# Down of the later chunks as three float32r products, up and down in quarters, third weight parts kept in DRAM

## The chip, the cores and the metric

The kernel runs on one core of a Trainium2 chip. The metric is device time in microseconds, lower is better. The engines are TensorE (PE, its weight loads shown as PEld), VectorE (DVE), ScalarE (ACT), GpSimd (POOL) and SyncE (SP), which issues nearly all DMAs. Each executes its own instructions in order and waits on semaphores for the others. SBUF is the on-chip memory, PSUM holds the sums of TensorE in banks.

## The reference

A mixture of two blocks: an mLSTM cell over 768 positions for 4 batches and 8 heads of 40, and then a GELU layer with 2048 hidden features.

```python
for t in range(S):                       # cell; B, H, S, D = 4, 8, 768, 40
    m_new = np.maximum(f_gate[:, :, t] + m, i_gate[:, :, t])
    f_stab = np.exp(f_gate[:, :, t] + m - m_new)
    i_stab = np.exp(i_gate[:, :, t] - m_new)
    m = m_new
    C = f_stab[..., None, None] * C + i_stab[..., None, None] * np.einsum('bhd,bhe->bhde', vt, kt)
    n = f_stab[..., None] * n + i_stab[..., None] * kt
    h_tilde = np.einsum('bhde,bhe->bhd', C, qt)
    denom = np.maximum(np.abs(np.einsum('bhd,bhd->bh', n, qt)[:, :, None]), 1.0)
    y[:, :, t] = sigmoid(o_gate[:, :, t]) * h_tilde / denom
x = y.transpose(0, 2, 1, 3).reshape(B * S, H * D)      # 3072 x 320
h = x @ w_in                                           # 320 x 2048  ("up")
g = 0.5 * h * (1.0 + erf(h / sqrt(2)))
return g @ w_out                                       # 2048 x 320  ("down")
```

## The kernel before

The 768 positions are cut into six chunks of 128, so a chunk has 4 x 128 = 512 tokens, a tile of 128 for each batch. Within a chunk the cell is computed by matrices: scores of q and k (`scores_two`, into tile `ps`), weighted by exponents of the gates (tile `W`: the row `M_d` is loaded by `load_M`, masked on POOL by `mask`, turned into exponents on ACT by `weights`), what comes from earlier chunks (`read_two`, tile `pf`, and the new state in `update_two`), and the values (`values`, tile `ph`). `finish` divides by the denominator, `turn_y` transposes y into `px` and `split_x` makes the three parts of the layer's input. q and k come through a DRAM copy (`copy_chunk`, `kq_d`) and `load_blocks`, and are transposed on DVE by `turn_k` and `turn_q`.

A float32 matmul takes two records in the profile. Up of the later chunks avoids it: x and w_in are each split into a high and a low part of type float32r plus a third one, and the sum of three products (high x high, low x low, rest x sum) stands for the float32 product. The third weight part, high + low, is made anew on DVE for each chunk (`join_weight`, L827) into a few buffers (`w_mid`). `up` does this in four pairs: `pair(0)`, `pair(1)`, `rest(0)`, then `pair(2)`, `pair(3)`, `rest(1)`. 16 blocks of 128 hidden features come out as tiles `pu`, and `out` applies gelu on ACT (L1036) into `g`.

Down of chunks 1 to 4 is one Strassen-like step: seven products of half the size instead of eight, in float32 (`down_steps`, matmuls at L1137), with sums of g's halves made on DVE (`hidden_sums`, L864 to L866, and `sum_late`, L1163), sums of the weights made once (`weight_sum`) and adds of the results (L1148). Down of the first chunk is a plain float32 product (`first_down_steps`, L1116). Down of the last chunk is already three float32r products (`LastDown`, matmuls at L991): gelu writes `g_whole`, ACT makes the high part (`split_hi`, L974), DVE the low one and the rest (`split_lo`, L977 and L978).

The order of the work is written out by hand. A step is a letter with a number; `play` walks through the words of an order and emits the step's instructions on all engines. `FRONT` holds the first two chunks of the cell, the conversion of the weights (`K` is `conv_one` on ACT, `J` is `conv_two` on DVE, which also fetches the next piece) and the first down (`F`, one row of w_out for all four tiles). Then, for each chunk, `up` is emitted as a whole, and `DOWN` mixes the products `F` of its down with the steps of the next chunk's cell. Since every engine runs in order, a word's place says what stands behind it. SP is a queue too: a DMA that waits for a buffer to be free holds all later ones.

Of the kernel before, what the change touches and what calls it, by code (L numbers as in the profile page):

```python
# [16 lines left out]
P = 128  # L17
# [14 lines left out]
    K V3 X1 J K r F J h8 h9 F F K F F F F F J K X2 G3 F F J K J F J K Y3 K B10 R1 X3 F p R2 J R3 F F J F F"""  # L32
DOWN = """
    M0 F Z F L3 W0 M1 W1 S0 C0 F F h0 Q2 F K2 G1 D3 B3 V0 G2 M2 W2 M3 W3 V1 K3 Q3 F G0 S2 Y0 G3 C2 h2 F
    F Y1 X0 V2 V3 F N F j R0 Y2 Y3 X1 F F X2 R1 F R2 X3 R3 F"""
# [3 lines left out]
def kernel(  # L39
# [34 lines left out]
    HELD = 7  # L74
    WP = 512
# [20 lines left out]
    w_out = const.tile([P, NF, DM], F32, name="w_out", tag="w_out")  # L96
# [28 lines left out]
    right_d = dram.tile([P, DFF // P // 2, DM // 2], F32, name="right_d")  # L125
# [95 lines left out]
    def warm(n):  # L221
        cold = ps_h.tile([P, P], F32, name="cold", tag="h")
        for _ in range(n):
            nc.tensor.matmul(cold, w_out[:, 0, 0:P], w_out[:, 0, 0:P], start=True, stop=True, skip_group_check=True)

    def fill(n):
        cold = ps_h.tile([P, P], F32, name="cold", tag="h")
        for i in range(n):
            r = quarters[i % 4]
            nc.tensor.matmul(cold[r, 0:D1], w_out[:, 0, r], w_out[:, 0, 0:D1], start=True, stop=True, skip_group_check=True)  # L230

    nc.vector.memset(w_out[:, 0, 0:P], 0.5)
# [116 lines left out]
    for f in range(NF):  # L349
        pieces.append(([w_src["out"][f * P:(f + 1) * P, :]], w_out[:, f, :]))  # L350
# [53 lines left out]
    later_loads = []  # L404
# [20 lines left out]
    class Cell:  # L425


        def __init__(self, c):
            self.c = c

            self.engine = nc.vector if c < 2 else nc.gpsimd
            self.finished, self.turned, self.reads = [], [], []
            self.qT, self.kT, self.vw, self.far, self.hs, self.px = {}, {}, {}, {}, {}, {}
# [43 lines left out]
        def load_last(self, b):  # L477

            self.by_block = fars[0].tile([P, NP, 2, L], F32, name="blocks3", tag="x_lo", bufs=1)
            for r in (32, 96):  # L480
                nc.gpsimd.memset(self.by_block[r:r + 32], 0.0)
            load_blocks(self.c * B + b, self.by_block)

        def last_M(self, b):
            load_M(self.c * B + b, self.before.t[:, 0:HF, P:2 * P])

        def turn_half(self, b, i):
            src = by_block if b < B - 1 else self.by_block
# [7 lines left out]
        def turn_q(self, b):  # L496
            self.turn_half(b, 1)
            if b < B - 2:
                load_blocks(self.c * B + b + 1, by_block)
            if self.c < NCH - 1 and b < B - 1:  # L500
                self.weigh_values(b)

        def load_next(self):
            if self.c + 1 < NCH:
                load_blocks((self.c + 1) * B, by_block)
            if self.c + 2 < NCH:
                copy_chunk(self.c + 2)

        def weigh_last(self, b):
# [36 lines left out]
        def scores_two(self, b0):  # L546

            two_b = (b0, b0 + 1)
            ps = [[pool.tile([P, NP, L], F32, name="ps", tag=tag) for hip in range(2)] for pool, tag in ((ps_mm, "a"), (ps_tr, "tr"))]
# [15 lines left out]
        def carry(self, b):  # L565
# [35 lines left out]
            self.read(b)  # L601

        def read_two(self, b0):

            c, two_b = self.c, (b0, b0 + 1)
            banks = self.banks = [ps_h.tile([P, H + NP, D1], F32, name="pf", tag="h") for _ in range(2)]
# [8 lines left out]
        def update_two(self, b0):  # L615

            c, two_b, banks = self.c, (b0, b0 + 1), self.banks
            if c + 1 < NCH:
                for i, b in enumerate(two_b):
                    vw = self.vw.pop(b)  # L620
                    for p in range(NP):
                        for hip in range(2):
                            nc.tensor.matmul(banks[i][used[hip], H + p, :], kb[turn_of(c * B + b)][:, 2 * p + hip, 0:D],  # L623
                                             vw[:, 2 * p + hip, :], start=True, stop=True)
            for i, b in enumerate(two_b):
                if b == B - 1:
                    self.far[b] = qb[2].rearrange("p h d -> p (h d)")[:, 0:H * D1].rearrange("p (h d) -> p h d", d=D1)
                else:
                    self.far[b] = fars[0].tile([P, H, D1], F32, name="far", tag="hs", bufs=2)
# [4 lines left out]
                if c + 1 < NCH:  # L634
                    st, d = state[b][:, :, 0:D1], dec[:, c - 1, b * NP:(b + 1) * NP].unsqueeze(2).to_broadcast([P, NP, D1])
                    nc.gpsimd.tensor_tensor(out=st, in0=st, in1=d, op=OP.mult)
                    for r in used:
                        nc.vector.tensor_tensor(out=st[r], in0=st[r], in1=banks[i][r, H:H + NP, :], op=OP.add)
                self.read(b)

        def read(self, b):

            self.reads.append(b)
            if self.c > 1 and self.reads.count(b) == 2:
                if b == 0:
                    load(self.c * B + NQ, 1, 3)
                else:
                    later_loads.append(lambda: load(self.c * B + b + NQ, 1, 3))

        def values(self, b):  # L650
# [3 lines left out]
            pool, tag = (ps_mm, "a") if self.c > 1 else (ps_h, "h")  # L654
# [5 lines left out]
            if self.c > 1 and b > 0:  # L660
                later_loads.append(lambda: load_M(n + NW))
            self.read(b)
# [6 lines left out]
        def finish(self, b):  # L669
# [3 lines left out]
            if self.c > 1:  # L673
                nc.scalar.activation(out=den, in_=hs[:, :, D], func=AF.Abs)
                nc.gpsimd.tensor_scalar(out=den, in0=den, scalar1=1.0, scalar2=None, op0=OP.max)
            if self.c < 2:
                nc.vector.scalar_tensor_tensor(out=y, in0=y, scalar=1.0, in1=hs[:, :, 0:D], op0=OP.add, op1=OP.mult)
            else:
                nc.gpsimd.tensor_tensor(out=y, in0=hs[:, :, 0:D], in1=y, op=OP.mult)
            if self.c < 2:  # L680
# [16 lines left out]
        def turn_y(self, b):  # L697
            n, t = self.c * B + b, slice(b * L, (b + 1) * L)
            if self.c > 0:
                px = ps_tr.tile([P, NX + 1, L], F32, name="px", tag="tr")  # L700
            else:
                px = ps_mm.tile([P, NX + 1, L], F32, name="px", tag="b")
# [18 lines left out]
            else:  # L721
                later_loads.append(lambda: load(n + NLD, 3, 4))
# [10 lines left out]
    HF, HT, HD = NF // 2, TG // 2, DM // 2  # L733

    Bm = [[lambda j, e=e, n=n: w_out[:, HF * e + j, HD * n:HD * (n + 1)] for n in range(2)] for e in range(2)]
    w_sums, parts, fars, w_hi, w_lo, w_mid = [], {}, [], {}, {}, {}
    T = {1: lambda j: w_sums[0][:, j, :], 2: lambda j: w_sums[1][:, j, :], 3: Bm[0][1]}
# [80 lines left out]
    def join_weight(i):  # L825
        w_mid[i] = raw.tile([P, 2, WP // 2], F32R, name="w_in_mid", tag="pow") if i % 5 in (1, 4) else w_f(F32R, "w_mid")
        nc.vector.tensor_tensor(out=w_mid[i], in0=w_hi[i], in1=w_lo[i], op=OP.add)  # L827

    def weight_sum(n):
        if n == 1:  # L830
            both = fars[0].tile([P, 2, HF, HD], F32, name="w_sums", tag="w_sums")
            w_sums.extend([both[:, 0], both[:, 1]])
        x, y = {1: (Bm[0][1], Bm[0][0]), 2: (Bm[1][1], T[1]), 3: (Bm[1][1], Bm[0][1])}.get(n) or (Bm[1][0], T[2])
        if n == 4:

            parts = {}

            def t4(j):
                if j // 3 not in parts:
                    parts[j // 3] = raw.tile([P, 3, HD], F32, name="t4", tag="pow" if j > 5 else "sig")  # L840
                return parts[j // 3][:, j % 3, :]

            T[4] = t4

        def step(j):
            nc.vector.tensor_tensor(out=T[n](j), in0=x(j), in1=y(j), op=OP.subtract)

        return [lambda j=j: (step(j), step(j + 1)) for j in range(0, HF, 2)]

    class Hidden:  # L850


        def __init__(self, summed):
# [416 lines left out]
```

## Time and profile before

| | us |
|---|---|
| median of 3 runs (lowest, highest) | 455.23 (454.81, 456.16) |
| span of the profiled execution | 453.3 |
| granted TensorE clock, mean | 1.000 |
| first down starts (chain) | 85.9 |
| chunk 1, 2, 3, 4, 5 start (first up matmul) | 121.0, 190.4, 260.3, 329.8, 397.0 |
| seven float32 products of a chunk, L1137 (chain) | 31.6 |
| three float32r products of the last chunk, L991 (chain) | 26.3 |
| one chunk of up (chain) | 26.5 |

The times of runs are medians of whole executions. The span is that of one profiled execution, from the first to the last instruction, and all durations are taken from it. A row of the groups gives a line, an engine, the tiles, how many there were, the busy time and the mean of one. A row of the timeline gives start, duration and what was merged; consecutive instructions of one engine overlap a little, so that the distance of two starts is shorter than a duration.

### The profile page before, as it was taken

To read this page: it belongs to the slowest core of one execution; us is meant where nothing else is said; L and a number is where in the kernel's file an instruction comes from. 1 tells how busy PE (TensorE), PEld (TensorE's weight loads), DVE (VectorE), ACT (ScalarE), POOL (GpSimd) and SP (SyncE) were. 2 spreads that over 40 slices of the span, in tenths; PEclk is the share of its full clock that TensorE was granted. 3 is DMA by queue.
4 is the path that set the end of the run, shared out by engine and by line. 5 is a ranking of instruction groups with operands and counts; after the bars stand their busy time and mean duration, and the time that the engine had idled before them with its cause. 6 is when DMAs were issued, how large, how long until landed. Compare 5 with 4: busy or idle time off the path is not lost.

```text
span 453.3 us, 13140 instructions
## 1 busy us (share of the span) xinstructions
PE 444.2 (98%) x5440; PEld 393.2 (87%) x5440; DVE 314.7 (69%) x672; ACT 238.2 (53%) x541; POOL 77.3 (17%) x117
## 2 busy tenths in 40 slices
PE   8899999999999999999999999999999999999996
PEld 7787888777788999988999988899988899988996
DVE  8797688877269688735578656488645577699940
ACT  4999999764231791221791203693203594247701
POOL 3002030000100443101433101533001513000000
PEclk9999999999999999999999999999999999999999
DMA  7999874886265644149834139942019930200001
GB/s 156 235 211 229 191 212 88 240 246 162 75 153 124 108 63 111 45 92 212 137 55 111 45 57 221 126 88 23 25 47 208 151 81 4 88 30 0 1 1 59
DMA packets 174876, 51.12 MB, mean 113 GB/s; under 512 B 154752, under 2 KB 168352, under 8 KB 174816
## 3 DMA queue, kind: packets, MB, share of 16 engines
q1 hardware_dynamic: 174496, 49.95, 50.5%
q8 instruction: 43, 0.70, 0.6%
q10 hardware_dynamic: 320, 0.33, 0.2%
q14 instruction: 17, 0.14, 0.1%
HBM read 45.47 MB, written 10.03 MB: 122 GB/s over the span
## 4 chain that ended last, share of the span: by engine, by line
PE 88%; ACT 6%; DVE 2%; DMA 1%; SPq 1%; issue 1%; DVEq 0%; ACTq 0%
PE po L1137 27%; PE pu L1021 23%; PE po L1116 8%; PE pu L1032 6%; PE po L991 6%; PE ph L659 3%; PE ps L557 3%; ACT W L465 2%; PE pu L810 2%; PE pf L612 2%; PE px L706 2%; PE pu L877 2%; PE pf L623 1%; SPq L151 1%; DMA bits<-in_moe_w_in_dram 1%
## 5 line engine op out<-in xcount | busy, mean ns | idle before, releaser
L1036 ACT ACTIVATE g<-pu 128x512 f32<-128x512 f32 x64 | 32.2, 618 | 81.2 <-PE pu L1032 81.2
L1137 PE MATMUL po<-w_out,g 128*128 128x160 f32 x512 | 74.4, 302 | 0.0
L1137 PEld LDWEIGHTS po<-w_out,g 128*128 128x128 f32 x512 | 70.1, 190 | 1.9 <-ACT g L1036 1.3
L1021 PE MATMUL pu<-x_hi,w_in_hi 128*128 128x512 f32 x160 | 39.0, 387 | 0.0
L465 ACT ACTIVATE W<-W,aT 128x128 f32<-128x128 f32 x128 | 38.6, 388 | 0.1
L439 POOL TENSOR_SCALAR_AFFINE_SELECT W<-W 128x1024 f32<-128x1024 f32 (+2 forms) x20 | 25.0, 1254 | 77.9 <-DMA W<-M_d 77.3
L1137 PE MATMUL po<-w_sums,sums 128*128 128x160 f32 x256 | 36.9, 302 | 0.0
L1137 PEld LDWEIGHTS po<-w_sums,sums 128*128 128x128 f32 x256 | 35.0, 190 | 0.4
L1116 PE MATMUL po<-w_out,g 128*128 128x320 f32 x128 | 34.9, 432 | 0.0
L1021 PEld LDWEIGHTS pu<-x_hi,w_in_hi 128*128 128x128 f32 x160 | 29.5, 189 | 5.7 <-ACT g L1036 1.3
L1116 PEld LDWEIGHTS po<-w_out,g 128*128 128x128 f32 x128 | 24.1, 190 | 9.7
L563 DVE TENSOR_TENSOR W<-ps,W 128x256 f32<-128x256 f32 (+1 forms) x48 | 18.1, 416 | 18.3 <-PE ps L557 7.1
L1021 PE MATMUL pu<-x_all,w_mid 128*128 128x512 f32 x80 | 30.3, 379 | 0.0
L1021 PE MATMUL pu<-x_all,w_in_mid 128*128 128x512 f32 x80 | 30.3, 379 | 0.0
L528 POOL TENSOR_TENSOR vw<-vb,ewT 128x328 f32<-128x328 f32 x12 | 9.2, 777 | 114.3 <-DMA vb<-in_v_dram 71.8
L864 DVE TENSOR_TENSOR sums<-g 128x512 f32<-128x512 f32 x16 | 12.8, 801 | 21.8 <-ACT g L1036 21.8
L384 DVE SCALAR_TENSOR_TENSOR pow<-sig,pow 128x320 uint32<-128x320 uint32 (+1 forms) x26 | 15.5, 597 | 7.2 <-ACT pow L373 7.2
L695 ACT COPY y_rest<-ob 128x128 f32<-128x128 f32 x16 | 4.7, 294 | 29.3 <-DVE ob L688 21.1
L372 ACT ACTIVATE sig<-bits 128x320 f32<-128x320 f32 (+1 forms) x26 | 15.1, 582 | 9.2 <-DMA bits<-in_moe_w_out_dram 4.4
L1021 PE MATMUL pu<-x_lo,w_in_lo 128*128 128x512 f32 x80 | 18.9, 379 | 0.0
L1021 PE MATMUL pu<-x_lo,w_in 128*128 128x512 f32 x80 | 18.9, 379 | 0.0
L1137 PE MATMUL po<-t,g 128*128 128x160 f32 x128 | 18.7, 299 | 0.0
(220 smaller groups left out, 960.8 us busy)
## 6 DMA issues: line engine op xcount, KB each, us to landing
W<-M_d SPq DMA_DIRECT2D x16, 512.0 KB, 5.2
bits<-in_moe_w_in_dram SPq DMA_DIRECT2D x20, 256.0 KB, 4.8
bits<-in_moe_w_out_dram SPq DMA_DIRECT2D x16, 320.0 KB, 4.5
blocks<-kq_d SPq DMA_DIRECT2D x32, 128.0 KB, 3.6
ob<-in_o_gate_dram SPq DMA_DIRECT2D x24, 160.0 KB, 4.6
out_dram<-o_sb SPq DMA_DIRECT2D x36, 80.0 KB, 1.9
kq_d<-in_k_dram SPq DMA_DIRECT2D x32, 80.0 KB, 2.4
kq_d<-in_q_dram SPq DMA_DIRECT2D x32, 80.0 KB, 2.5
```

The source lines that it names most:

```text
L372: nc.scalar.activation(out=s, in_=hi.bitcast(F32), func=AF.Copy, scale=2.0 ** -112)
L384: nc.vector.scalar_tensor_tensor(out=p, in0=s, scalar=3, in1=p, op0=OP.logical_shift_left, op1=OP.bitwise_or)
L439: nc.gpsimd.affine_select(out=x, in_=x, compare_op=OP.is_ge, fill=1.0e30, base=base, pattern=[[0, H], [1, x.shape[2]]], channel_multiplier=-1)
L465: nc.scalar.activation(out=W[n][:, h, :], in_=src, func=AF.Exp, scale=-1.0, bias=aT[:, self.c, r:r + 1])
L557: nc.tensor.matmul(ps[i][hip][halves[x ^ i], p, t], kT[i][r, p, halves[x]], qT[i][r, p, t], start=True, stop=True)
L563: nc.vector.tensor_tensor(out=w[r, :, t], in0=ps[i][hip][r, :, t], in1=w[r, :, t], op=OP.mult)
L991: nc.tensor.matmul(in_pairs(po[t]), x[:, t * L:(t + 1) * L], in_turns(w), start=(f, k) == first, stop=(f, k) == last, skip_group_check=True)
L1021: nc.tensor.matmul(in_pairs(pus[i][e]), w[k][:, e, i * P:(i + 1) * P], in_turns(x[:, k, :]), start=(n == 0 and k == 0), stop=False, skip_g ...
L1032: nc.tensor.matmul(in_pairs(pu[e]), w[r, i // 2, i % 2 * P:(i % 2 + 1) * P], in_turns(x[r, NX, :]), start=False, stop=(n == 2), skip_group ...
L1036: nc.scalar.activation(out=g.t[:, HF * e + i, :], in_=pu[e], func=AF.Gelu, scale=4097.0)
L1116: nc.tensor.matmul(po[b], g.t[:, f, b * L:(b + 1) * L], w_out[:, f, :], start=(f == 0), stop=(f == NF - 1))
L1137: nc.tensor.matmul(bank[k][:, t, :], lhs(j, t), rhs(j), start=(first and t == 0 and j == 0), stop=(t == 1 and j == HF - 1), skip_group_che ...
```

## The change

Down of chunks 1 to 4 takes the form of the last chunk, and all five chunks share one pair of classes, `Later` (weights) and `Chunk` (one chunk).

- w_out is held in four tiles of four rows each, in the order `feature`, so that each can be taken over by something else once its rows are used. The high parts of its rows (`a`, ACT) and the low parts (`b`, DVE) are made once, in the front, and stay in SBUF.
- The third parts are made once and stored to DRAM: those of w_out on POOL in chunk 1 (`y`), with four slots in SBUF that are reloaded for each chunk (`o`); those of w_in by `z` (the first five on DVE, the others on POOL), with five slots that are reloaded (`i`), ten tiles per chunk.
- Up goes in four quarters (`U0` to `U3`) of four feature blocks, each with its rest. Each block's gelu (`g`) gives the whole, the high part on ACT and the other two on DVE, into a ring of five slots of three parts. The products of one block (`d`) are 12 matmuls into four banks that hold for the whole chunk. `E` copies those banks out, in the next chunk.
- `U1` to `U3` and the next chunk's cell share four banks, `U0` and the products the other four; the pairs swap from chunk to chunk.
- Steps with a number of 4 or more belong to the chunk after the next. Letters as in `CELL`: M mask, W weights, G gate, V values, Y finish, X `turn_y`, R `split_x`, K and Q transposes, D weighing, C `read_two`, S `scores_two`, h `update_two`; L loads q and k blocks, B the row of M, J k and v, O the output gate, `+` copies a chunk of q and k.

The diff, cut:

```diff
-    K V3 X1 J K r F J h8 h9 F F K F F F F F J K X2 G3 F F J K J F J K Y3 K B10 R1 X3 F p R2 J R3 F F J F F"""
-DOWN = """
...
+    K V3 X1 J K r F J h8 h9 F a0 a1 F K b0 b1 F a2 a3 F b2 b3 F F F J K X2 G3 F F J K J Y3 F J K a4 a5 b4 b5 a6 b6 K B10 R1 F X3 a7 b7 F Z Z p R2 J R3 +
+    a8 b8 F J Z a9 a10 <0 <1 >0 >1 a11 a12 a13 a14 a15 z0 z1 b9 b10 b11 b12 b13 b14 b15 F F """
+CELL = "MWGVYXRKQDCSh"
+LATER = """
+    U0 E0 E1 W0 W1 E2 E3 K1 Q1 L2 g0 g1 g2 g3
+    U1 i5 i6 i7 i8 i9 g4 d0 g5 o4 d1 g6 o5 d2 g7 o6 S0 d3 o7 M2 W2 G0 G1 G2 G3 + K2
+    U2 i10 i11 D0 D1 g8 d4 g9 o8 d5 g10 o9 d6 g11 C0 h0 Q2 V0 V1 B3 L3 J0 o10 d7 o11 J1 D2 Y0 Y1 K3 Q3 L4 M3
+    U3 i12 i13 i14 g12 d8 g13 o12 d9 g14 o13 d10 g15 W3 D3 S2 o14 d11 o15 C2 h2 V2 V3 B4 B5 B6 J2 J3 Y2 Y3 X0 R0 d12 o16 X1 R1 d13 o17 X2 R2 d14 o18 X3 R3 d15 o19
+    K4 M4 M5 O0 O1 O2 O3 Q4 L5"""
+
+SECOND = """
+    z2 U0 z3 z4 K0 Q0 L1 g0 g1 g2 g3 y0 y1 y2 y3 z5 z6 K1 Q1 L2
+    U1 g4 d0 g5 y4 d1 g6 y5 d2 g7 y6 S0 d3 y7 z7 z8 z9 K2
+    U2 i10 i11 D0 D1 g8 d4 g9 y8 d5 g10 y9 d6 g11 + C0 h0 G0 G1 G2 G3 M2 W2 Q2 V0 V1 B3 L3 J0 y10 d7 y11 J1 D2 Y0 Y1 K3 Q3 L4 M3
+    U3 i12 i13 i14 g12 d8 g13 y12 d9 g14 y13 d10 g15 W3 D3 S2 y14 d11 y15 C2 h2 V2 V3 B4 B5 B6 J2 J3 Y2 Y3 X0 R0 d12 o16 X1 R1 d13 o17 X2 R2 d14 o18 X3 R3 d15 o19
...
+LAST = """
+    U0 E0 E1 E2 E3 g0 g1 g2 g3 U1 i5 i6 i7 i8 i9 x g4 d0 g5 o4 d1 g6 o5 d2 g7 o6 d3 o7
...
+        def g_parts(self, n):
+
+            i = 3 * (n % NM)
+            return [self.ring[:, i + k, :] for k in range(3)]
...
+        def join(self, i):
+
+            (nc.vector if i < NM else nc.gpsimd).tensor_tensor(out=self.mid_home(i), in0=w_hi[i], in1=w_lo[i], op=OP.add)
+            nc.sync.dma_start(out=w_in_mid_d[i], in_=self.mid_home(i).bitcast(F32))
+
+        def load_in(self, i):
+
+            nc.sync.dma_start(out=self.mid_home(i).bitcast(F32), in_=w_in_mid_d[i % (2 * NM)])
...
+        def out_mid(self, n):
...
+            nc.gpsimd.tensor_tensor(out=self.w_mid[n % 4], in0=self.w_hi[n], in1=self.w_lo[n], op=OP.add)
+            nc.sync.dma_start(out=w_out_mid_d[n], in_=self.w_mid[n % 4].bitcast(F32))
...
+        def load_out(self, n):
+            nc.sync.dma_start(out=self.w_mid[n % 4].bitcast(F32), in_=w_out_mid_d[n % NF])
+
+    class Chunk:
...
+        def gelu(self, n):
+
+            whole = raw.tile([P, TG], F32, name="g_whole", tag="sig")
+            hi, lo, rest = self.later.g_parts(n)
+            nc.scalar.activation(out=whole, in_=self.pus[n // 4][n % 4 // 2][n % 2], func=AF.Gelu, scale=4097.0)
+            nc.scalar.activation(out=hi, in_=whole, func=AF.Copy, scale=PART)
+            nc.vector.scalar_tensor_tensor(out=lo, in0=whole, scalar=-1.0 / BASE, in1=hi, op0=OP.mult, op1=OP.add)
+            nc.vector.tensor_tensor(out=rest, in0=whole, in1=hi, op=OP.subtract)
+
+        def product(self, n, t, k):
+            x, w = self.later.g_parts(n)[k], self.later.w_parts(n)[k]
+            nc.tensor.matmul(in_pairs(self.po[t]), x[:, t * L:(t + 1) * L], in_turns(w), start=(n == 0 and k == 0),
+                             stop=(n == NF - 1 and k == 2), skip_group_check=True)
+
+        def down(self, n):
+
+            if n == 0:
+                self.po = [pool.tile([P, DM], F32, name="po", tag=tag) for pool, tag in self.main for _ in range(2)]
+            for k in range(3):
+                for t in range(B):
+                    self.product(n, t, k)
...
+        def finish(self, t):
...
+            nc.scalar.activation(out=self.o_sb[:, t % 2, :].rearrange("p (a i) -> p a i", a=2),
+                                 in_=self.po[t].rearrange("p (i a) -> p a i", a=2), func=AF.Copy, scale=4097.0)
+            send(self.c, t, self.o_sb[:, t % 2, :])
```

In the cell, `update_two` adds to the state after all its `far` products, and `finish` of batches 2 and 3 of the later chunks does the maximum and the first product on DVE instead of POOL and ACT. Loads that hung on steps of the cell are steps of their own.

395 lines of the change are left out of this document (138 added, 257 removed).

## The prediction

> **What bounds the kernel now.** I read the page first, then the waits of PE, the chain, the groups with shapes kept apart, and a table by stage.
>
> ```profile
> span 453.3 us, 13140 instructions
> ## 1 busy us (share of the span) xinstructions
> PE 444.2 (98%) x5440; PEld 393.2 (87%) x5440; DVE 314.7 (69%) x672; ACT 238.2 (53%) x541; POOL 77.3 (17%) x117
> ...
> PE 88%; ACT 6%; DVE 2%; DMA 1%; SPq 1%; issue 1%; DVEq 0%; ACTq 0%
> ```
>
> PE is busy nearly always and holds 88% of the chain. In the waits of PE the longest is 1.1 us, at the start; after that nothing reaches 0.6:
>
> ```profile
> PE pt L519 <- DMA kb<-in_k_dram: 1.1, 1, 1.1
> ...
> PE ph L659 <- issue: 0.5, 1, 0.5
> ```
>
> The stages, from the chain, with their starts: first down 85.9, then chunks 1 to 5 at 121.0, 190.4, 260.3, 329.8 and 397.0. The row of chunk 2 in the table by stage (length, then busy time of PE, PEld, DVE, ACT, POOL):
>
> ```profile
> 190.40:260.30 69.90, 69.33 (x957) 63.40 (x956) 44.51 (x89) 29.72 (x71) 17.29 (x24) 1.00 0.53 107
> ```
>
> PE has no slack; DVE has 25 us and ACT 40. So work taken off PE counts in full, until a wait appears. What down costs now, and what it costs in the form that the last chunk already has:
>
> ```profile
> 286.82 4.54 PE po L1137 x32
> ...
> 423.47 26.29 PE po L991 x192
> ```
>
> **The change, part by part.** *Down.* In the chain, the L1137 rows of one chunk (260.33 to 329.82) add up to 4.54 x4 + 4.35 + 2.37 x2 + 2.18 + 2.17 = 31.6 us: 112 float32 matmuls of 160 columns, two records each, 224 x 0.141. The new form is the last chunk's, 16 x 4 x 3 = 192 matmuls of 128x320 in 26.29 us, 0.137 each. That is 5.3 us less of PE per chunk, in chunks 1 to 4: **-21.2 us**. Up keeps its 144 matmuls (10.36 + 2.79 + 10.56 + 2.79 = 26.5 us, a quarter 6.6), the cell its 11.3 (69.4 - 26.5 - 31.6), the last chunk its 52.8.
>
> *DVE.* Per chunk go ten joins (L827, 10 x 0.69), twelve half-sums (L864 to L866, 4 x (0.80 + 0.74 + 0.91)), two late sums (2 x 1.48) and five adds (5 x 0.49): 22.1 us. In come 16 x (0.69 + 0.69) = 22.1 (rows L977, L978). Nothing won or lost in sum, but the new work stands between a gelu and the products that follow it at once.
>
> *ACT.* Per chunk come 16 high parts, 16 x 0.64 = 10.2 us, and four copies of 0.44 that replace others. 30 + 10 + two more table loads of 1.28 is 43 of some 66 us: still hidden. What matters is the pace: in the last chunk gelu and high part alternate like this,
>
> ```profile
> 421.56 0.60 ACT L965 ACTIVATE g_whole<-pu 128x512 f32<-128x512 f32 x1 [4.83 <-PE pu L1032]
> 422.19 0.63 ACT L974 ACTIVATE g_part<-g_whole 128x512 fp32r<-128x512 f32 x1
> 422.73 0.58 ACT L965 ACTIVATE g_whole<-pu 128x512 f32<-128x512 f32 x1
> ```
>
> 1.17 us for one feature block, where PE needs 1.64 for its products (26.29 / 16). But a ring of five slots makes the high part of block n wait for the products of n-5, and two buffers of whole values make a gelu wait for DVE two blocks back. So I placed a later chunk by hand, time from the start of U0, with the durations above:
>
> - U0 and U1 fill PE to 13.2. ACT does E0, E1 (0.8), W0, W1 (16 exponents, 4.78 in the row at 223.18), E2, E3 and a table load, done at 8.0, so g3 has read its bank at 12.1, in time for d0. But K1, Q1 (1.3 of DVE) stand ahead of g0, and their blocks (L5) are issued only behind o19 and O0 to O3: some 2.6 us after U0 begins, four issues (3.3 in the row at 233.67) and landing, near 9 to 10. Bounds: 0 if that is early, 1.4 if it ends at 10; I take **0.5**, nearer the early row.
> - g7 must wait for d2, so S0's eight products on DVE (1.41 per four) leave U2's first banks 0.6 late: **0.6**. Bounds 0 and 0.8.
> - g13, g14, g15 wait for d8, d9, d10; W3 comes behind g15 on ACT, with a table load: done at 53.7. S2 is over at 50.6, d11 at 52.3. C2 waits 0.7, V2 0.1, X0 0.9, since DVE must finish the second half of S2 and then h2 before X0's bank is free: **1.7**. Behind C2 in PE's order stand h2, V2, V3 and X0, none of which can pass it. Bounds 0.5 (if W3 went early) and 3.
>
> That is 2.8 in chunks 2 and 3, 2.5 in chunk 4, where the cell has no update, and 2.3 in chunk 1, where W0 and W1 lie in the front.
>
> *Chunk 1 alone.* The third parts of down are made on POOL (16 x about 0.9, from L528 0.78 and L679 0.98) and half of those of up (5 x about 1.4, scaled from the same rows to 512): 21 us more of POOL, with 24 stores. PE needs each only a quarter later, so I cost the making at nothing; if that cover went, every late one would cost its 0.9. The copies of chunk 3 (16 DMAs) now stand behind y9's store, which needs d5. In before they take
>
> ```profile
> 239.50 1.23 SPq L159 DMA_DIRECT2D kq_d<-in_q_dram  x2
> ```
>
> per pair, so some 10 us: y9's store at 33, copies to 43 or 45, B3, L3 and its landing (3.6) at about 49. K3 and Q3 wait for that on DVE, and g12's parts stand behind them; they would have run at 45. Bounds 0 (the copies land early or DVE has other work) and 5.4 (the whole delay, through g15's bank to S2 and X0); I take **4.0**, near the late end, for every row on the way is measured. Chunks 2 and 3 issue their copies before U2 and pay nothing.
>
> *DMA.* Each later chunk reloads ten tiles of 256 KB and sixteen of 160 KB: 5.2 MB in 66 us, 79 GB/s on top of the 89 to 108 of the stages; 246 is seen on the page. Landing: 4.8 us for 256 KB (bits, L362). The closest one is i5: behind L2, which waits for Q1, it is issued near 14.2 and lands near 19; U2 needs it at 22.7. Cover 3.5 us, so cost nothing; a late one costs its lateness once per chunk.
>
> *The front.* ACT gains 16 high parts (x 0.5), three splits (1.9), W0, W1 and a load (6.1): 16 us, on 17.5 busy of 35 from 86 to 121. DVE gains 16 x 0.49 + 2.1 + 1.4 = 11.3 on 21.5. Both fit; U1, 6.6 us after U0, is the first that needs ACT's last copies. Cost 0, bounds -0.5 and +4.
>
> **Sum.** 453.3 - 21.2 + 0.5 x 0 (front) + (2.3 + 4.0) + 2.8 + 2.8 + 2.5 = 446.5 us of span. The runs' median is 455.2, 1.9 above this span: **448.4 us**.
>
> **Rivals.** *The row behind the second of them*: where POOL works, two-input DVE instructions stretch:
>
> ```profile
> 218.77 2.69 POOL L439 TENSOR_SCALAR_AFFINE_SELECT W<-W 64x1024 f32<-64x1024 f32 x2
> ...
> 219.36 1.58 DVE L866 TENSOR_TENSOR g<-g 128x512 f32<-128x512 f32 x1
> ...
> 222.64 0.69 DVE L866 TENSOR_TENSOR g<-g 128x512 f32<-128x512 f32 x1
> ```
>
> [...]
>
> *A, the order holds almost everywhere*: the 14.4 us of waits shrink to 3 (the low bounds above, 0.5 for each chunk's end and a little beside): 453.3 - 21.2 + 3 + 1.9 = **437**. For it: after the start PE in before waits at no place over 0.6. Against: the ring of five and W3's place are in the order itself.
>
> *B, POOL stretches DVE in chunk 1.* 21 us more of POOL beside DVE that is busy some 46 of 66 us: 21 x 0.7 x (1.58/0.69 - 1 = 1.3) would be 19 us of DVE, of which its idle 20 take most; if a third lands on PE, +6: **454**, no change. Against: the masks that stretched L866 are another instruction of POOL.
>
> *C, slower: the reloads run late.* SP is one queue in order: i5 stands behind L2, and L2 behind Q1 and L5. Should Q1 end 3.5 us later than placed, U2 waits for tile 5's third part and everything behind it on SP (o4 to o7, which d4 to d7 need) slides too. At a landing of 4.8 us per chunk and four chunks: 448.4 + 19.2 = **467.6**. It decides above 6.8 us, 1.7 per chunk. For it: SP waits on PE at each of 16 reloads and on DVE at four loads a chunk, and each holds what is behind it. Against: DMA is busy only 0.46 to 0.53 in these stages.
>
> *D, the clock.* The granted clock is 1.00 in every stage, with no PE gap over 1.5 us. Chunk 1's gap near S2 could be 4 us. If the clock fell for it and PE lost as much time again before it is back, +4: **452**.
> [...]
>
> **Chances.** Forecast 0.45, its own range 441 to 453; A 0.23; B 0.10; D 0.05; C 0.17. The whole range, leaving out half of A's lower end and most of C: **437 to 459**. Faster by over 0.3% (1.4 us, about what a measurement here can tell): 0.45 + 0.23 + 0.05 + 0.04 of B = 0.77; same 0.05; slower 0.18.
>
> **What would show it.** Right: four runs of 192 po records, 26.3 us each, chunks 2 and 3 of about 67 us, and DVE or ACT named ahead of C2, X0 and U2. The front right: chunk 1 still begins near 121. Chunk 1 right: DVE's K3 waiting for blocks, S2 late by some 4 us, chunk 1 near 70. C: PE waiting for a DMA of a third part at U2, d4 or d12. B: L1074 and L1075 well above 0.69 while POOL is busy. Wrong would be chunks 2 and 3 at 69 or more, or PE idle at a step that I have placed without a wait.

## The result, and the profile after

| | before | after |
|---|---|---|
| median of 4 runs each (lowest, highest), us | 455.70 (454.81, 457.12) | 474.06 (472.21, 477.17) |
| span of the profiled execution, us | 453.3 | 472.4 |
| granted TensorE clock, mean | 1.000 | 0.981 |
| length of chunks 1, 2, 3, 4, 5, us | 69.4, 69.9, 69.5, 67.2, 56.3 | 77.5, 76.3, 70.8, 69.4, 57.2 |

The changed kernel is slower: ratio 1.041, 95% interval 1.036 to 1.045. The prediction, 448.4 in a range of 437 to 459, was wrong, and with it the sign.

The head of the page after, its row of the granted clock over 40 slices, and its chain:

```profile
span 472.4 us, 13340 instructions
...
PE 441.2 (93%) x5312; PEld 381.1 (81%) x5312; DVE 317.3 (67%) x655; ACT 288.3 (61%) x613; POOL 81.4 (17%) x114
...
PEclk9999999999999997999999799999999999899999
...
PE 72%; DVE 8%; ACT 7%; issue 5%; SPq 4%; DMA 3%; DVEq 0%; ACTq 0%
```

PE's busy time is only 3 us less than before (444.2), and its share of the chain fell from 88% to 72%. The 7, 7 and 8 in the row of the granted clock (tenths of full speed) have no counterpart before, where all 40 slices were at 9. The table by stage shows where (length, busy time of PE, PEld, DVE, ACT, POOL, then clock, DMA share and GB/s):

```profile
121.20:198.70 77.50, 68.84 (x926) 61.06 (x925) 58.28 (x108) 39.17 (x80) 38.69 (x41) 0.96 0.69 176
198.70:275.00 76.30, 69.27 (x927) 61.69 (x926) 47.84 (x99) 41.19 (x88) 13.85 (x20) 0.96 0.72 175
275.00:345.80 70.80, 66.39 (x926) 58.86 (x925) 47.40 (x97) 41.03 (x88) 11.26 (x16) 1.00 0.72 175
```

Chunks 1 and 2 have a clock of 0.96, and PE is idle for 8.7 and 7.0 us of them (length less busy time), where in before it was idle for 0.1 and 0.6. The traffic went from 108 to 176 GB/s. The waits of PE (total, times, longest) name the new idle time:

```profile
PE ph L652 <- issue: 9.5, 5, 3.0
PE ps L562 <- ACT g_whole L1072: 7.9, 6, 5.2
PE po L1079 <- issue: 2.7, 1, 2.7
PE po L1079 <- ACT g_whole L1072: 2.1, 4, 0.8
```

Two kinds. The first and third, 12.2 us, are "issue": PE waits for no engine and no transfer that the profile shows. The second and fourth are gelus that come late.

*The issue waits.* One of them in PE's timeline, at the end of chunk 2's cell (start, duration, the idle time before in brackets):

```profile
255.83 0.81 PE L1079 MATMUL po<-w_out_hi,g_parts 128*128 128x320 f32 x4
...
257.66 1.14 PE L615 MATMUL pf<-state,qT 64*64 64x41 f32 x64
258.73 0.81 PE L626 MATMUL pf<-vw,kb 128*40 128x41 f32 x32
259.47 1.51 PE L652 MATMUL ph<-vb,W 128*32 128x41 f32 x123
264.03 0.35 PE L652 MATMUL ph<-vb,W 128*32 128x41 f32 x5 [3.05 <-issue]
264.32 0.69 PE L695 MATMUL px<-ident,ob 128*128 128x128 f32 x2
264.80 0.42 PE L695 MATMUL px<-ident,y_rest 128*128 128x128 f32 x1
264.87 1.41 PE L1079 MATMUL po<-w_out_hi,g_parts 128*128 128x320 f32 x4
266.08 1.27 PE L1079 MATMUL po<-w_out_lo,g_parts 128*128 128x320 f32 x4
```

PE stops inside V3, five matmuls short of its end, with every input there. Count PE's records from the start of the program: a weight load and a matmul are one each, and so is each of the 160 semaphore and drain instructions that the page does not count. Then all six such stops are before record 256n + 193, so they lie whole multiples of 256 apart; none of the six other PE waits of over 0.6 us is at such a record. A queue of its own ("instruction" in the table of DMA queues) moved 42 pieces in this run, each of 16 KB, where PE has 10784 records: one for every 256. In before it moved 43, for 10973 records. So I take a piece for the refill of PE's instructions; the trace names the queue and not what the pieces hold. The times of these pieces beside the six stops, where a block is 256 records and a stop is the distance of the starts of the records on both sides of it, and the pieces are given to the blocks in order:

```
PE enters  piece of the next block   PE runs on  stop   whole block
186.23     187.5 to 188.5            189.76      1.5    3.5
236.56     238.5 to 239.4            240.74      2.9    4.2
259.26     261.8 to 262.7            264.03      3.2    4.8
311.53     313.1 to 314.0            315.36      2.0    3.8
333.55     335.0 to 336.0            337.42      1.9    3.9
401.55     402.9 to 403.9            405.24      2.0    3.7
```

At these six places the transfer of the next block begins 1.3 to 2.5 us after PE has entered the block ahead of it and takes about 1 us, and PE goes on 1.3 to 1.4 us after it has landed. So such a block took 3.5 to 4.8 us. Two value steps, V2 and V3, are 128 weight loads and 128 matmuls, exactly one block, and the matmuls of V3 in chunk 3 run in 1.7 us beside the stop (1.07 and 0.65 in the chain).

The 3.5 us are no floor, for the piece does not always begin so late. Taken in order, 16 of the 42 pieces began before PE entered the block, by up to 3.4 us. Two blocks of this run, entered inside the cell's short steps at 157.05 and 381.58, passed in 2.04 and 1.81 us without a stop; there the piece had begun 1.0 and 0.8 us ahead. In before the same steps stood apart between products of down. Four blocks there passed in 2.5 to 3.5 us, with one stop among them, of 0.7.

*The clock.* In the timeline above, the four high products behind V3 take 1.41 us, where those in the row at 255.83 take 0.81. Windows of 2 us around it, PE alone (length, busy, clock, DMA share, GB/s):

```profile
260.00:262.00 2.00, 0.98 (x90) 1.00 0.76 236
262.00:264.00 2.00, 0.00 (x0) 0.80 0.45 172
264.00:266.00 2.00, 1.97 (x12) 0.50 0.24 59
266.00:268.00 2.00, 2.00 (x10) 0.50 0.93 272
268.00:270.00 2.00, 2.00 (x10) 0.50 0.71 119
```

A stop of 3.05 us, and the clock stands at half for 6.8 us behind it. The records of the clock show three such stretches before the end: 6.8 us from 177.9 (in the wait of 5.24 us at S2, below), 6.8 from 263.2, 3.4 from 406.6. Before the last two of them the longest gap of PE was 3.05 and 1.8 us.

*The late gelus.* S2 in chunk 1, on PE, and what DVE did in that time:

```profile
173.77 0.44 PE L562 MATMUL ps<-qT,kT 64*64 64x128 f32 x4
179.45 0.68 PE L562 MATMUL ps<-qT,kT 64*64 64x128 f32 x2 [5.24 <-ACT g_whole L1072]
181.19 2.19 PE L562 MATMUL ps<-qT,kT 64*64 64x128 f32 x45 [1.06 <-ACT g_whole L1072]
```

```profile
176.28 0.71 DVE L506 STREAM_TRANSPOSE kT<-blocks 128x512 f32<-128x512 f32 x1 [8.86 <-DMA blocks<-kq_d]
176.92 0.67 DVE L506 STREAM_TRANSPOSE qT<-blocks 128x512 f32<-128x512 f32 x1
177.51 0.65 DVE L1074 SCALAR_TENSOR_TENSOR g_parts<-g_whole,g_parts 128x512 fp32r<-128x512 f32 x1
...
179.28 1.23 DVE L1075 TENSOR_TENSOR g_parts<-g_whole,g_parts 128x512 fp32r<-128x512 f32 x1
180.43 1.35 DVE L1074 SCALAR_TENSOR_TENSOR g_parts<-g_whole,g_parts 128x512 fp32r<-128x512 f32 x1
```

DVE sat 8.86 us at K3 for the blocks of L3, with the parts of g12 behind it. L3 was issued at 169.43, behind twelve us of copies on SP (156.84 to 168.7). The place is the one forecast.

### The profile page after: what moved, and what is told of

Read it like the earlier page. It is cut to its first block, busy times and chain, and to the rows that moved or that the text cites. A ratio compares the mean times of both kernels' runs of the same rounds, so it can differ in the third digit from the quotient of the medians.

```text
span 472.4 us, 13340 instructions
## 1 busy us (share of the span) xinstructions
PE 441.2 (93%) x5312; PEld 381.1 (81%) x5312; DVE 317.3 (67%) x655; ACT 288.3 (61%) x613; POOL 81.4 (17%) x114
## 4 chain that ended last, share of the span: by engine, by line
PE 72%; DVE 8%; ACT 7%; issue 5%; SPq 4%; DMA 3%; DVEq 0%; ACTq 0%
PE po L1079 25%; PE pu L1059 18%; PE po L958 6%; PE pu L1065 5%; PE ph L652 4%; PE ps L562 3%; DMA blocks<-kq_d 2%; PE pu L788 2%; PE px L695 2%; SPq L186 2%; DVE g_parts L1075 2%; PE pf L615 2%; ACT g_whole L1072 2%; SPq L170 2%; PE pu L817 2%
## 5 line engine op out<-in xcount | busy, mean ns | idle before, releaser
L1072 ACT ACTIVATE g_whole<-pu 128x512 f32<-128x512 f32 x80 | 47.5, 594 | 82.2 <-PE pu L1065 56.8
L1074 DVE SCALAR_TENSOR_TENSOR g_parts<-g_whole,g_parts 128x512 fp32r<-128x512 f32 x80 | 58.7, 734 | 56.3 <-ACT g_parts L1073 54.9
L1079 PE MATMUL po<-w_out_mid,g_parts 128*128 128x320 f32 x320 | 59.6, 303 | 0.0
L1075 DVE TENSOR_TENSOR g_parts<-g_whole,g_parts 128x512 fp32r<-128x512 f32 x80 | 57.9, 724 | 0.0
L1073 ACT ACTIVATE g_parts<-g_whole 128x512 fp32r<-128x512 f32 x80 | 50.5, 631 | 4.7 <-PE po L1079 2.3
L1079 PE MATMUL po<-w_out_hi,g_parts 128*128 128x320 f32 x240 | 49.6, 323 | 2.7 <-issue 2.7
L1079 PEld LDWEIGHTS po<-w_out_mid,g_parts 128*128 128x128 f32 x320 | 49.4, 193 | 0.0
L1079 PE MATMUL po<-w_out_lo,g_parts 128*128 128x320 f32 x240 | 45.5, 305 | 0.0
L1079 PEld LDWEIGHTS po<-w_out_lo,g_parts 128*128 128x128 f32 x240 | 37.5, 194 | 0.0
L958 PEld LDWEIGHTS po<-w_out,g 128*128 128x128 f32 x128 | 23.9, 190 | 10.5 <-DVE w_out L410 1.2
```

The costliest lines, as they stand in the source:

```text
L958: nc.tensor.matmul(po[b], g.t[:, f, b * L:(b + 1) * L], w_row(n), start=(n == 0), stop=(n == NF - 1))
L1072: nc.scalar.activation(out=whole, in_=self.pus[n // 4][n % 4 // 2][n % 2], func=AF.Gelu, scale=4097.0)
L1073: nc.scalar.activation(out=hi, in_=whole, func=AF.Copy, scale=PART)
L1074: nc.vector.scalar_tensor_tensor(out=lo, in0=whole, scalar=-1.0 / BASE, in1=hi, op0=OP.mult, op1=OP.add)
L1075: nc.vector.tensor_tensor(out=rest, in0=whole, in1=hi, op=OP.subtract)
L1079: nc.tensor.matmul(in_pairs(self.po[t]), x[:, t * L:(t + 1) * L], in_turns(w), start=(n == 0 and k == 0), stop=(n == NF - 1 and k == 2), s ...
```

## The experiments

Each is compared with runs of the kernel before on the same chip (medians 454.9 to 456.0). The first four have two runs each, the others four to twelve. "Issue stops" are PE's stops at record 256n + 193 of 0.6 us or more, measured as in the table above less 0.1 us each, summed; in the changed kernel they are 12.8 us. "Issue waits" are PE's idle times of that name, 12.2 us there.

**Without the reloads.** `load_in` and `load_out` issue nothing.

```diff
         def load_in(self, i):
-            nc.sync.dma_start(out=self.mid_home(i).bitcast(F32), in_=w_in_mid_d[i % (2 * NM)])
...
         def load_out(self, n):
-            nc.sync.dma_start(out=self.w_mid[n % 4].bitcast(F32), in_=w_out_mid_d[n % NF])
```

> The 90 or so reloads of third weight parts (L1003, L1039) are left out, so the last four chunks use stale third parts; the 26 stores and everything else stay. Theory F (TensorE runs out of instructions: all six gaps named issue in the changed kernel begin at its instruction record 256 n + 193, where it enters the next 16 KB of its stream, in the dense small matmuls of the cell): the gaps become a little shorter, as DMA is lighter, but four or more of the six stay, 8 us or more of 12.2; total 466 to 471 us. Rival R (the added DMA traffic delays the work, by the reloads themselves or by what stands behind them on SP): the gaps fall under 2 us in sum and the total comes to 452 to 458 us.

Measured: 460.23 us, ratio 1.010 (1.003 to 1.018), span 459.2. The waits of PE:

```profile
PE ps L562 <- ACT g_whole L1074: 8.0, 3, 5.2
PE ph L652 <- issue: 5.4, 4, 1.8
PE po L1081 <- issue: 1.3, 1, 1.3
```

Between the two expectations. The issue stops are still at the same five places of chunks 2 to 4 and at record 193, but shorter: 7.4 us, as such a block now passes in 3.0 to 3.3 us (one in 3.95); the sixth, in chunk 1, is down to 0.2. The pieces take as long as before (0.9 to 1.2 us). What is shorter is the time from PE's entry until the piece begins, 0.8 us on average at the six places instead of 1.7. The longest wait for issue is 1.8 us, and only chunk 1's stretch of half clock is left. So the reloads cost some 14 us, and not by landing late: beside them the pieces begin 0.9 us later and the stops are 5.4 us longer in sum, and with them two stretches of half clock (6.8 and 3.4 us) stand behind stops, where without them none does. These two make up most of the 14 us. The bursts remain a loss without the reloads.

**Down steps among the values.**

```diff
-    ... Q2 V0 V1 B3 L3 J0 o10 d7 o11 ...
+    ... Q2 V0 d7 V1 B3 L3 J0 o10 o11 ...
-    ... C2 h2 V2 V3 ... X0 R0 d12 o16 X1 R1 d13 ...
+    ... C2 h2 V2 d12 V3 ... X0 R0 o16 d13 X1 R1 ...
```

> Only the order on TensorE changes: d7 between V0 and V1, d12 between V2 and V3, then X0 d13 X1 d14 X2 X3 d15. Theory F: the 256 records between two entries last longer than the 3.5 to 4.8 us that a refill took, the issue gaps fall from 12.2 us to under 5, the half-clock stretches of chunks 2 and 4 go with them (3.0 and 1.7 us), total 460 to 466 us. Rival R: the gaps only move, 10 us or more of them stay, total 471 to 476 us.

Measured: 469.03 us, ratio 1.030 (1.019 to 1.041). The waits of PE:

```profile
PE ps L562 <- ACT g_whole L1072: 7.0, 5, 4.4
PE ph L652 <- issue: 4.0, 4, 2.3
PE po L1079 <- DMA w_out_mid<-w_out_mid_d: 2.1, 1, 2.1
```

The issue waits fell from 12.2 to 4.0 us with the same transfers, as expected, but the time missed its 460 to 466. Part of the gain went into new waits: d12 now comes earlier than its third part in chunk 3, whose reload stands behind L4 and i12 to i14 on SP, and waits 2.1 us for it, with 3.4 us of half clock behind that. The stretch of chunk 4 went, that of chunk 2 shrank to 3.4 us.

**Copies later in chunk 1.** `+` of SECOND moved from behind g11 to behind Q3.

```diff
-    U2 ... d6 g11 + C0 h0 ... K3 Q3 L4 M3
+    U2 ... d6 g11 C0 h0 ... K3 Q3 + L4 M3
```

> In chunk 1 alone, the 16 copies of chunk 3 are issued behind Q3 and ahead of L4, and no longer ahead of B3 and L3. If L3's place behind the copies is what makes K3 and S2 late, the TensorE waits of 5.2 and 1.1 us at S2 in chunk 1 go to under 1, with the half-clock stretch there (2 us): 465 to 468 us, chunk 1 near 70. If the stores or POOL hold it as well: 470 to 474.

Measured: 477.03 us, ratio 1.047 (1.040 to 1.055): missed. The longest waits of PE:

```profile
PE ph L652 <- issue: 9.8, 5, 3.1
PE po L1079 <- ACT g_whole L1072: 8.3, 3, 7.0
```

The stop at S2 is gone, but the copies now delay L4 and L5, so that K1 of the next chunk and, behind it on DVE, the parts for d0 are 7.0 us late, with 10 us of half clock. The cause of the stop was right, and twelve us on an in-order queue do not vanish by going elsewhere.

**Blocks earlier.** K4, Q4 and L5 right behind V3 and B4, so that L5 no longer waits behind o19 and O0 to O3.

```diff
-    ... V2 V3 B4 B5 B6 ...
-    K4 M4 M5 O0 O1 O2 O3 Q4 L5
+    ... V2 V3 B4 K4 Q4 L5 B5 B6 ...
+    M4 M5 O0 O1 O2 O3
```

> K4, Q4 and L5 come right behind V3, so that L5 is issued some 10 us before the next U0 instead of 3.5 us after it. The wait of VectorE for blocks at the start of chunks 2 to 5 (9.6 us in chunk 3) falls under 1 us, and the TensorE waits at d0 and S0 behind it (1.3 us in chunk 2, 1.0 in chunk 3) go: 1 to 3 us off the total, 471 to 473. If K4 and Q4 on VectorE delay the last finishes and X2 instead, no gain or 1 us more.

Measured: 469.41 us, ratio 1.031 (1.022 to 1.039). The waits of d0 in chunks 2 and 3 are gone and the span is 3.8 us shorter, somewhat more than expected; 11.2 us of issue waits remain.

**The three moves together**, with the copies cut into single batches of 3 us at four places of SECOND.

```diff
-    z2 U0 z3 z4 K0 Q0 L1 g0 g1 ...
+    z2 U0 z3 z4 K0 Q0 L1 + g0 g1 ...
-    U2 i10 i11 D0 D1 ... g11 + C0 h0 ...
+    U2 i10 i11 + D0 D1 ... g11 C0 h0 ...
-    U3 i12 i13 i14 g12 ... y14 d11 y15 C2 h2 V2 V3 ...
+    U3 i12 i13 i14 + g12 ... y14 d11 y15 + C2 h2 V2 d12 o16 V3 ...
```

> All three moves together: Down steps between the values (d7 behind V0, d12 behind V2, d13 and d14 between the split outputs), K4, Q4 and L5 right behind V3, and the copies of a chunk cut into single batches of 3 us each, in SECOND set where the SP queue stood idle (behind L1, i11, i14 and y15). The reloads of o10, o11 and o16 to o18 are issued one step earlier. Theory O (the loss of the changed kernel lies in where the steps stand: three separate waits, each with its own place): the 6 us at S2 in chunk 1 with its half clock go, the 1 us waits of d0 go, the issue gaps fall from 12 us to 4 or less, no stretch of half clock before the end: 454 to 460 us, about the time before. Rival N (the reloads are there, so each wait removed comes back elsewhere, as in the single moves): 465 to 470 us, no better than the best single move.

Measured: 459.75 us, ratio 1.011 (1.008 to 1.015). Theory O by its time, just. Issue stops 2.3 us; S2 in chunk 1 still waits 0.7 + 2.0 us (with 3.4 us of half clock, which the theory had gone), and the transposes of y now wait 3.3 us in three chunks for DVE's finish, since fewer products of down stand between V3 and them.

**Values in halves**, everything else as in the changed kernel.

```diff
-                for r in halves if self.c == 0 else quarters:
+                for r in halves if self.c != 1 else quarters:
```

> Values of chunks 2 to 5 in two column groups instead of four: 32 matmuls of 16 heads x 2 groups in place of 64... counted in records of the trace, 64 a batch instead of 128, with order, transfers and results as in the changed kernel. Theory R (PE runs out of instructions: a burst of short records outruns the refill of 256 records): V0 with V1 is half a refill instead of a whole one, the issue gaps fall from 12 us to 5 or less, they still begin at record 193 of 256, and the half clock behind V3 in chunks 2 and 4 goes: 464 to 469 us, although a batch itself takes some 0.3 us longer. Rival W (the gaps are a wait of the values for their weights or inputs that the profile does not show): gaps of 2 to 3 us stay at the values, at other record numbers, 473 to 477 us.

Measured: 461.77 us, ratio 1.015 (1.011 to 1.020), span 460.3. The same place in PE's timeline:

```profile
257.27 0.81 PE L626 MATMUL pf<-vw,kb 128*40 128x41 f32 x32
257.92 1.92 PE L652 MATMUL ph<-vb,W 128*64 128x41 f32 x59
260.96 0.37 PE L652 MATMUL ph<-vb,W 128*64 128x41 f32 x5 [1.13 <-issue]
```

One word of the source takes 12 us off. V2 and V3 now have 64 matmuls instead of 128, the issue stops went from 12.8 to 1.3 us, and with them both stretches of half clock behind V3. Order and transfers are the same, so it is the number of instructions that made the stops. This is theory R, with a larger effect than it was given; rival W is out, as the values waited for no data.

**Traffic in the kernel before.** Unused transfers beside each product of down, first on SP's queue, then on ACT's.

```diff
+    def read_again():
+        spare = dram.tile([P, 512], U32, name="spare_in")
+        nc.sync.dma_start(out=spare, in_=w_src["in"][0:P, 0:512])
+        spare = dram.tile([P, DM], U32, name="spare_out")
+        nc.sync.dma_start(out=spare, in_=w_src["out"][0:P, 0:DM])
```

> The kernel before, with one 256 KB and one 160 KB transfer from the weights in DRAM to a spare place in DRAM issued on the SP queue behind each of the 14 products of Down (5.8 MB a chunk, about what the reloads move; nothing reads them). Theory R (traffic lengthens a refill, but a loss comes only where short records stand close together): the cell steps of this kernel stand between products of 1.3 us or more, so no issue gap over 1 us and no half clock before the end: 455 to 459 us. Rival D (the traffic alone costs it, in whatever order): 464 us or more, as the 14 us between the changed kernel and the one without reloads.

> The kernel before with the same unused transfers as e7_traffic_in_before (14 of 256 KB and 14 of 160 KB a chunk), but issued on ACT's queue, so that no load of SP stands behind them. Theory Q (what cost 18 us there was the SP queue: the loads of M and blocks behind the extra issues came late): 456 to 462 us, no wait of PE over 2 us, issue gaps at record 193 of 256 of about 1 us at most. Rival D (it is the traffic itself, which slows every transfer and refill): 466 us or more, with the same waits of 6 us.

Measured: 473.47 us, ratio 1.044 (1.038 to 1.049), and 481.29 us, ratio 1.055 (1.052 to 1.058). Both theories missed, and by their times alone both runs would be rival D's. But neither answers the question, as in both the cell's own loads came late. On SP's queue the loads of the cell came late behind the extra issues; the largest wait, in chunk 4, on DVE:

```profile
385.01 1.41 DVE L563 TENSOR_TENSOR W<-ps,W 128x256 f32<-128x256 f32 x4 [1.93 <-PE ps L557]
392.61 1.75 DVE L563 TENSOR_TENSOR g<-ps,g 128x256 f32<-128x256 f32 x4 [6.18 <-DMA spare_out<-in_moe_w_out_dram]
```

On ACT's queue SP's own copies stood still instead, with nothing of the extra on SP:

```profile
137.31 1.19 SPq L159 DMA_DIRECT2D kq_d<-in_q_dram  x2
151.28 1.19 SPq L159 DMA_DIRECT2D kq_d<-in_k_dram  x2
156.38 1.19 SPq L159 DMA_DIRECT2D kq_d<-in_q_dram  x2
```

and the blocks behind them made S0 wait 8.2 us. SP's own waits name what held it: in the whole run its copies (L159) wait 29.9 us, in ten waits, for the landing of `spare_in` and 18.1 us, in three, for that of `spare_out`. All these transfers take eight semaphores (101 and 103 to 109) in turn, and those waits of SP are for the last transfer on the copy's own semaphore. The copy at 151.28 uses number 108, as does the `spare_in` that ACT issued only at 147.78, behind a product. So a second queue did not keep the extra transfers out of SP's way. What both runs do show: with 5.8 MB more a chunk, no stop at record 193 in this order is over 1.3 us, and on SP's queue all of them together are 3.0 us.

**The best order, with halves**: K4, Q4 and L5 as in the fourth experiment, the copies as in the fifth, values in halves, and in SECOND K3, Q3 and L4 behind g13 so that the parts of g12 and g13 do not stand behind the late blocks.

```diff
-    U2 ... J1 D2 Y0 Y1 K3 Q3 L4 M3
-    U3 i12 i13 i14 g12 d8 g13 y12 ...
+    U2 ... J1 D2 Y0 Y1 M3
+    U3 i12 i13 i14 + g12 d8 g13 K3 Q3 L4 y12 ...
```

> Values in halves, K4, Q4 and L5 right behind V3, the copies cut into single batches at four places of SECOND, and in SECOND K3, Q3 and L4 behind g13 instead of behind Y1; the places of the Down steps among the values are those of the changed kernel. Theory O (the three places explain the loss: the burst at the values, the late blocks at S2 of chunk 1, the late blocks at d0): from the 460.3 us span of the kernel with halves, the 6.6 us at S2 and its stretch of half clock (6.8 us, so 3.4 us lost) and 3 us at d0 go: a span of 447 to 451 us, a time of 448 to 453 us, 1 to 2 per cent under the time before, and no half clock before the end. Rival N (something comes in their place, the floor under the traffic is that of the two best kernels so far): 456 to 461 us.

Measured: 452.58 us (451.62 to 454.67, 6 runs) against 455.16, ratio 0.993 (0.991 to 0.995): 0.7 per cent faster than before, where 1 to 2 were expected, and 21 us faster than the changed kernel. The profiled execution, the longest of the six, has a span of 452.9. Its page and stages 1 to 3:

```profile
PE 437.3 (97%) x4800; PEld 378.2 (83%) x4800; DVE 314.7 (69%) x655; ACT 288.8 (64%) x613; POOL 81.6 (18%) x114
```

```profile
122.00:191.30 69.30, 67.37 (x797) 60.20 (x796) 58.62 (x108) 39.05 (x80) 36.02 (x37) 1.00 0.71 179
191.30:263.00 71.70, 67.95 (x799) 59.88 (x798) 46.64 (x99) 41.41 (x88) 12.57 (x18) 1.00 0.78 186
263.00:330.50 67.50, 66.64 (x798) 59.29 (x798) 47.70 (x99) 41.16 (x88) 12.80 (x18) 1.00 0.78 187
```

In this execution the clock is 1.00 throughout, with all reloads in place at 179 to 187 GB/s. Theory O holds but for chunk 2, which keeps one stop of 2.1 us at V3 and waits of 0.9 at d10 and 0.8 at S2.

**The halves alone, in before and taken out of the best order.**

> The kernel before with the values of chunks 2 to 5 in two column groups instead of four, nothing else. Theory R (the halves help only where bursts of short records outrun the refill, and before has no such gap): 454 to 458 us, same or up to 3 us slower, since a batch takes longer. Rival G (halves are a gain of their own, whatever the order): under 450 us, about 10 us less, as in the changed kernel.

> The kernel e8_together with the values of chunks 2 to 5 back in four column groups (128 records a batch), order and transfers as in e8. Theory R (the bursts at the values are a loss of their own, about 10 us with the half clock behind them): 461 to 467 us, issue gaps of 8 us or more in sum at record 193 of 256, half clock behind V3 of chunk 2 or 3. Rival P (the places of copies and blocks were the whole loss, the halves only helped the order of e6): 452 to 455 us.

Measured: before with halves 457.12 us, ratio 1.004 (1.002 to 1.006), so the halves by themselves cost 2 us; the best order with quarters 463.90 us, ratio 1.020 (1.016 to 1.024), with issue stops of 12.7 us and 3.4 us of half clock. The same edit costs 2 us where the cell steps stand apart and saves about 11 where they stand close together: theory R on both sides, and rivals G and P are out.

**LATER ordered as SECOND.**

```diff
-    U1 i5 ... i9 g4 ... G3 + + + + K2
-    U2 i10 i11 D0 D1 ... g11 C0 ... L3 J0 o10 d7 o11 ... K3 Q3 L4 M3
+    U1 i5 ... i9 + g4 ... G3 K2
+    U2 i10 i11 + D0 D1 ... g11 o10 C0 ... L3 J0 d7 o11 ... M3
+    U3 i12 i13 i14 + g12 d8 g13 K3 Q3 L4 ...
```

> e8_together with LATER ordered as its SECOND: the copies cut into four places, K3, Q3 and L4 behind g13, and o10 issued ahead of V0 (in e8 it stood behind L3 and d10 waited 0.9 us for it in chunk 2). The trace of e8 shows 4.5 us of such waits in chunk 2 (0.9 at d10, 0.8 at S2, 2.1 of issue at V3) and 1.1 in chunk 3. Theory: 2 to 4 us of them go, 448.5 to 451.5 us. Rival: the copies at four places run into the blocks and M loads of these chunks, 453 to 457 us.

Measured: 456.39 us, ratio 1.002 (0.999 to 1.004): the rival. The waits aimed at fell (issue 2.1 to 0.9), but U2 now waits for its third parts; in chunk 2 their first reload is issued at 212.46 instead of 210.79:

```profile
PE pu L1059 <- DMA w_in_mid<-w_in_mid_d: 4.2, 6, 1.5
```

## Why the prediction was wrong

The forecast put the chunks at 70.4, 67.4, 67.0, 64.4 and 56.3 us; they took 77.5, 76.3, 70.8, 69.4 and 57.2. That is 25.7 us more, and 0.2 more in the front.

- *The front at nothing* was right: chunk 1 begins at 121.2.
- *Down, -5.3 us a chunk.* Near in its rate: a run of 36 products takes 5.09 us, 1.70 for each block of 12, and 1.63 among the last ones, where 1.64 was counted. But PE's busy time in chunk 3 fell only from 69.4 to 66.4, where 64.1 was counted. The quarters double the changes between 128-row and 64-row weights (20 instead of 10 in all), each with 0.33 us in which no weights are loaded, and a block of products alone between other steps takes 1.83 (row in the chain at 297.20) instead of 1.64. Some 2 to 3 us a chunk that no term of the sum had. From start to start of the matmuls, chunk 3's down takes 27.9 us where 26.3 were counted, and up 0.5 to 0.8 more than before. So only half of the 21.2 us came: with the part of the half clock taken out, PE's busy time in chunks 1 to 4 fell by 10.6 us. It stays so in the best order, whose chunk 3 has 66.6.
- *The waits that I placed by hand.* d0: 0.5 a chunk, bounds 0 to 1.4, measured 1.1 and 0.8 in chunks 2 and 3; moving L5 removed it. S0: 0.6, measured 0.2. C2, V2 and X0: 1.7, bounds 0.5 to 3; nothing over 0.7 there. The hand-made schedule was good where it was drawn.
- *K3 in chunk 1*, 4.0 with a bound of 5.4: the place, the cause and the DVE wait for blocks were as written, the size was 5.24 + 1.06 = 6.3 us, plus about 2 for the half clock behind it. The copies took 11.9 us on SP instead of 10, and the four issues of L3 another 4.4.
- *The reloads cost nothing.* This is the step that failed, together with what it left out. I asked only whether a reload lands before its reader, and there the answer was right: PE waited for no third part (rival C did not come). But the sum had no term for the refill of PE's instructions. The new order packs them into bursts, and the refill begins later beside the reloads (1.7 us after PE's entry on average at the six stops, 0.8 at the same places without reloads): 12.2 us of stops in which no data is missing. The experiment without reloads gives 14 us for the traffic, the one with halves 12 us for the bursts, with the other cause left in place in each; they are not to be added, as each needs the other. The trace of before held a hint that I read past: the one wait of 0.5 at `ph`, "issue", with no engine to blame, stands at such a record 193 too.
- *Rival D*, the clock, at a chance of 0.05 and for chunk 1 only: that the clock falls for a gap was an assumption there, which no row of before shows. In the changed kernel it stood at half three times before the end, once where the rival put it, in the wait of 5.24 us at S2 in chunk 1, and twice behind issue stops, of 3.05 and 1.8 us. It costs about 6.8 us (half of PE's busy time of 4.2, 6.0 and 3.4 us in the three stretches).
- *Rival A* (the order holds) fell with the issue stops. *Rival B*: L1074 and L1075 took longer in chunk 1, where POOL is busy for 38.7 us, 0.90 and 0.89 us on average against 0.69 in chunk 2, where it is for 13.9. That is 6.6 us of DVE where 19 was the estimate. Two of them, 1.23 and 1.35 us at 179 to 181, stand in the wait at S2.

Added up, chunks 1 to 4 have 12.2 us of issue waits, 6.8 of half clock and 10.6 of matmuls that took longer than counted, less 4.8 of other waits that were counted and did not come; chunk 5 has 0.9 more. That is the 25.7 us.

With the three places mended and the reloads kept, 452.6 us lies in the likeliest case's own range (441 to 453), but in part by luck: chunk 3 takes 67.5 us there, where 67.0 was forecast, with 0.9 us of waits instead of the 2.8 placed and 2.5 us more of matmuls. So about half of the gain of the products was there; in the changed kernel it was given back in front of the values, at K3, and in the clock.

Left open: how much the traffic alone would cost the order of before, since both ways of adding it also held up SP; and why a refill begins 1.3 us after PE enters a block in one place, 2.5 in another, and up to 3.4 us ahead of it elsewhere. That the reloads delay it is shown by one experiment, which also took 100 issues off SP.

## What to carry to other kernels

Packing many short matmuls side by side was not free here even with all their data there: PE stood 12.2 us in six stops. So count the records of such a burst, and set its time against what a block of 256 took where the stops were (3.5 to 4.8 us with the reloads, 2.3 to 4.0 without), above all when the change also adds traffic. What helped here was a long step between two bursts (issue waits from 12.2 to 4.0 us) and fewer, wider matmuls (issue stops from 12.8 to 1.3). Waits of PE for "issue" at record numbers a multiple of 256 apart were that limit in this kernel; without the reloads they stayed at the same record number. Two stops with half clock behind them, of 3.05 and 1.8 us, cost about twice their length (another 3.0 and 1.7 us). And a faster form of one step is to be counted in the place where it will stand: the products were near their rate in long runs (1.63 to 1.70 us a block where 1.64 was counted), and lost half of their gain in short ones (1.83) and in the changes around them (0.33 each).

## What the runs showed that I had not expected

- What I take for the refill of PE's instructions: 42 pieces of 16 KB for 10784 records, one for 256. At the six stops a block took 3.5 to 4.8 us with the reloads and 2.3 to 4.0 at the same places without them; 1.3 to 1.4 of the former lie between landing and the next instruction. Two blocks whose piece began 1.0 and 0.8 us ahead of PE's entry passed in 2.04 and 1.81 us without a stop.
- The stretches of half clock in the changed kernel lasted 6.83, 6.83 and 3.41 us. Two of them stood behind stops of 3.05 us (at 261) and 1.8 (at 403), but none behind one of 2.73 at 238. In the best order with quarters there were seven waits for issue of up to 3.0 us and one stretch of 3.4: in these runs the length of the gap alone did not decide.
- A change between 128-row and 64-row weights in up cost 0.33 us on PE's weight loads here: 20 changes, 6.6 us in the changed kernel; 10 changes, 3.3 us in before.
